# Block 1 of a fused attention and SwiGLU kernel: the sums of h move to another place in VectorE's queue

## The chip, the cores and the metric

The kernel runs on one core of a Trainium2 chip. The metric is device microseconds (us) of one execution. Eight runs of the kernel before lie between 1035.02 and 1037.15 us, with a median of 1036.09 us.

## The reference

Two layers follow each other. The first is linear attention without softmax over batch 8, 8 heads, 576 positions and a head width of 64; the second is a SwiGLU feed-forward layer on 4608 rows of width 512 with 1536 hidden columns. All numbers are float32.

```python
kv = np.einsum('bhsd,bhse->bhde', k, v)
out = np.einsum('bhsd,bhde->bhse', q, kv)
x = out / rms(out) * g_norm            # rows (b, s), columns (h, d)
g = x @ w_gate
return (g * (1 / (1 + np.exp(-g))) * (x @ w_val)) @ w_out
```

## The kernel before

The 4608 rows are cut into 9 blocks of 512 rows (n = 0 to 8). For each block the kernel computes the product for the hidden layer ("up"), then the product with w_out ("down"), while the attention of the next block is filled into the down stage. The inner dimensions are multiplied by Strassen's method in Winograd's form: seven products p = 1 to 7 of halves take the place of eight. Block 0 is multiplied plainly, block 1 by one level of the method (class Up, L573), and blocks 2 to 8 by two levels (class Inner, L638). The change concerns block 1 alone.

In block 1, the 12 tiles of hidden columns are taken in 6 pairs, j = 0 to 5. In this text p3(2) is product 3 of pair 2, and so on. One product is 8 matmuls of 128x256. Products collect in three kinds of PSUM bank (L519): b takes products 1, 6, 7 and 4, a takes 2, and c takes 5 and then 3 on top. The order on TensorE is written out by hand in `sequence` (L590): for pair j, products 1 and 5 come first, then 4 and 3 of the pair before, then 6, 2 and 7.

After each product, engines other than TensorE read the bank:

- after 1, 6 and 7, ScalarE copies b into a scratch tile "r" (L567, L571, L601)
- after 2, VectorE adds bank a to the scratch (L597)
- after 7, VectorE adds bank c, which then holds product 5, to U3 (L605). This add is called U3(j). Product 3 of the same pair adds on top of bank c, so p3(j) can't start before U3(j) has read the bank
- after 4, ScalarE applies Silu (L609) and GpSimd multiplies one half of h (L610), called h1(j)
- after 3, VectorE adds bank c to U2 (L613), called U2(j), and GpSimd multiplies the other half of h (L614), called h2(j). Then `h_sums` (L932) makes two VectorE instructions of 128x256: s1 = a21 + a22, which reads what h1(j) wrote, and a21 = s1 - a11, which also reads what h2(j) wrote. The two together are called sums(j).

The results of the sums are read in block 1's down stage alone. GpSimd also subtracts weight tiles for the pairs to come (`prepare`, L581): three tiles "t" of 128x512 for each pair, out of a pool of 9. And block 1 has a third task: the second level's weight leaves for blocks 2 to 8 are made here (`leaf_steps`, L807) and written to DRAM. These are some 28 steps for each pair, four behind each product (L964): VectorE subtractions and additions on t, wg and wv, each with both operands in SBUF, and DMAs issued by SyncE. A tile t goes back to GpSimd when the DMA of its leaf has landed. For the last two pairs the leaves of wg and wv are left to the down stage (L636).

The framework places each instruction in its engine's queue by priority (the order in which the program makes them) and by when it expects the operands; `tc.issue_after` keeps an instruction behind another one on the same engine. On the chip each engine works its queue strictly in order. The lambdas at L111, L112 and L113 issue every add, subtract and multiply, so the profile shows those lines and one has to go by the tiles: "h<-s,h" on VectorE is the second instruction of the sums, "h<-r" on GpSimd is h1 or h2, "r<-c,r" on VectorE is U2 or U3, and "c<-x,wv" on TensorE is product 3.

Of the kernel before, what the change touches and what calls it, by code (L numbers as in the profile page):

```python
# [18 lines left out]
def kernel(  # L19
# [41 lines left out]
    nc = tc.nc  # L61
# [11 lines left out]
    NP = NF // 2  # L73
# [37 lines left out]
    add = lambda e, o, a, b: e.tensor_tensor(out=o, in0=a, in1=b, op=OP.add)  # L111
# [7 lines left out]
    class Words:  # L119
# [12 lines left out]
        def __init__(self, src, shape):  # L132
            self.raw = ld_pool.tile([P, LD], U32, name="ld")[:, 0 : 2 * BLK]
            dst = self.raw.rearrange("p (a b) -> p a b", a=shape[0])
            self.sent = nc.sync.dma_start(out=dst, in_=src)
            self.shape = shape
            self.begun = False
# [435 lines left out]
    class Up(Quad):  # L573
# [25 lines left out]
        def after7(self):  # L599
            self.u3 = self.piece(2)  # L600
            copied = nc.scalar.copy(out=self.u3, in_=self.ps["b"])  # L601

            with tc.issue_after(copied.ins):
                nc.scalar.activation(out=self.s, in_=self.s, func=ACT.Silu)
            add(nc.vector, self.u3, self.ps["c"], self.u3)  # L605

        def after4(self):
            g = self.piece(3)
# [3 lines left out]
        def after3(self):  # L612
            add(nc.vector, self.u2, self.ps["c"], self.u2)  # L613
            mul(nc.gpsimd, self.h[:, :, 0:HB], self.s, self.u2)  # L614
            self.ffn.ended = self.ffn.h_sums(self.j, 1, nc.vector)

        def multiply(self, p):
            super().multiply(p)
# [301 lines left out]
    class Ffn:  # L920
        def __init__(self, n, att):
            self.n, self.att = n, att
            self.h = h_pool.tile([P, NF, BLK], F32, name="h")
            self.ps, self.leaf_room, self.ended = {}, None, None

            self.making, self.later, self.latest = [], [], []

# [215 lines left out]
```

## Time and profile before

| what | value |
|---|---|
| median of 8 runs | 1036.09 us |
| the profiled execution | 1036.78 us |
| its span in the trace | 1035.0 us |
| up stage of block 1 | 160.4 to 241.2 us of the span |
| TensorE's clock in the execution | 1.00 of full speed |
| VectorE in 160 to 245 us, waiting for GpSimd's h | 10.0 us, 5 times |

The page of a profile has the busy time of each engine, its share in 40 slices of the span, and the groups of instructions by line. The timeline view lists an engine's instructions in order of time: the start, the duration, engine, line, operation, tiles written and read, and in brackets the idle time before it with what ended that. The view of waits gives for each pair of waiter and releaser the total, the count and the longest, in us. VectorE is pipelined: where instructions don't depend on each other, the next starts some 0.08 us before the one before it ends, so the price of one is the distance between starts.

### The profile page before, as it was taken

Reading aid. Unit: us, or ns where it says so; the run is one execution under the profiler, and the core shown is the slowest. Engines: PE = TensorE matmul, PEld = TensorE weight load, DVE = VectorE, ACT = ScalarE, POOL = GpSimd, SP = SyncE. Lnnn points to the kernel's source line nnn. Section 1 sums busy time; section 2 is a strip of 40 time slices with the busy share of each in tenths; the row PEclk is TensorE's granted clock in tenths of the full one; section 3 lists DMA queues with packets and bytes.
Section 4 is the critical chain, followed back from the end, with each engine's and each line's share of the span. In section 5 each row is a group of like instructions: output and inputs, shape, how many; then the busy total and the mean of one; then the engine's idle time right before and its main releaser. Section 6 shows DMA issues by size and latency. Waiting matters only on the chain.

```text
span 1035.0 us, 21447 instructions
## 1 busy us (share of the span) xinstructions
PE 1014.8 (98%) x8586; PEld 904.9 (87%) x8586; DVE 695.8 (67%) x1184; ACT 231.8 (22%) x362; POOL 368.7 (36%) x280
## 2 busy tenths in 40 slices
PE   5999999999999999999999999999999999999998
PEld 4544688878899989998999899988999899989997
DVE  2999596886756856575666666674669466856661
ACT  2665111222212211212111112111212111211110
POOL 0000443444025612463156305640455136513670
PEclk9999999999999999999999999999999999999999
DMA  7689704674678556855686468736872766067601
GB/s 214 198 268 259 150 1 127 178 201 93 187 206 243 111 110 213 242 146 103 187 249 170 66 203 239 202 51 181 242 196 53 168 197 194 22 155 215 189 29 42
DMA packets 247876, 168.15 MB, mean 162 GB/s; under 512 B 124640, under 2 KB 215904, under 8 KB 247776
## 3 DMA queue, kind: packets, MB, share of 16 engines
q1 hardware_dynamic: 221280, 163.36, 57.6%
q10 hardware_dynamic: 26432, 3.41, 2.1%
q8 instruction: 68, 1.11, 0.4%
q14 instruction: 32, 0.26, 0.1%
q0 software_dynamic: 64, 0.00, 0.0%
HBM read 138.02 MB, written 22.41 MB: 155 GB/s over the span
## 4 chain that ended last, share of the span: by engine, by line
PE 91%; DVE 4%; DMA 2%; issue 1%; ACT 1%; POOL 0%; SPq 0%; DVEq 0%; POOLq 0%; ACTq 0%
PE b L706 25%; PE b L551 20%; PE c L706 13%; PE c L551 10%; PE a L706 6%; PE a L551 5%; PE b L1008 4%; PE c L1008 4%; PE m L316 1%; PE m L357 1%; DMA h<-in_v_dram 1%; DVE xi L112 1%; DVE r L112 1%; DVE r L111 1%; DMA w<-t 1%
## 5 line engine op out<-in xcount | busy, mean ns | idle before, releaser
L111 POOL TENSOR_TENSOR r<-r 128x256 f32<-128x256 f32 (+1 forms) x105 | 110.9, 1063 | 310.2 <-DVE r L111 233.1
L111 DVE TENSOR_TENSOR r<-b,r 128x512 f32<-128x512 f32 (+1 forms) x273 | 162.1, 606 | 64.9 <-PE b L706 59.6
L112 POOL TENSOR_TENSOR t<-wo 128x512 f32<-128x512 f32 x81 | 115.4, 1449 | 194.4 <-DVE wo L111 106.0
L111 DVE TENSOR_TENSOR r<-c,r 128x512 f32<-128x512 f32 (+1 forms) x179 | 108.5, 618 | 94.7 <-PE c L706 55.5
L706 PE MATMUL b<-x,t 128*128 128x128 f32 x1092 | 151.1, 275 | 0.0
L706 PEld LDWEIGHTS b<-x,t 128*128 128x128 f32 x1092 | 136.5, 192 | 0.7 <-DVE r L111 0.2
L111 DVE TENSOR_TENSOR r<-a,r 128x512 f32<-128x512 f32 (+1 forms) x99 | 62.5, 631 | 106.2 <-PE a L551 62.9
L706 PE MATMUL c<-xi,t 128*128 128x128 f32 x840 | 112.2, 275 | 0.4 <-DVE xi L111 0.4
L113 POOL TENSOR_TENSOR h<-r 128x1024 f32<-128x1024 f32 (+1 forms) x40 | 81.3, 2047 | 82.5 <-DVE r L111 77.0
L706 PEld LDWEIGHTS c<-xi,t 128*128 128x128 f32 x840 | 102.8, 192 | 0.5 <-DVE xi L111 0.5
L551 PE MATMUL b<-wo,h 128*128 128x256 f32 x432 | 99.4, 382 | 0.1
L551 PE MATMUL b<-t,h 128*128 128x256 f32 x432 | 96.9, 381 | 0.0
L551 PEld LDWEIGHTS b<-t,h 128*128 128x128 f32 x432 | 81.3, 190 | 11.3 <-issue 0.2
L551 PEld LDWEIGHTS b<-wo,h 128*128 128x128 f32 x432 | 79.9, 190 | 12.7 <-DVE h L113 2.5
L720 ACT COPY r<-b 128x512 f32<-128x512 f32 x63 | 36.9, 586 | 212.1 <-PE b L706 205.3
L706 PE MATMUL b<-xi,t 128*128 128x128 f32 x588 | 79.9, 276 | 0.0
L706 PEld LDWEIGHTS b<-xi,t 128*128 128x128 f32 x588 | 72.4, 192 | 0.1
L706 PE MATMUL b<-x,wg 128*128 128x128 f32 x336 | 52.7, 279 | 0.2 <-DVE x L112 0.2
L706 PE MATMUL b<-x,wv 128*128 128x128 f32 x336 | 51.3, 275 | 0.0
L551 PE MATMUL c<-t,s 128*128 128x256 f32 x216 | 48.3, 380 | 0.0
L551 PE MATMUL a<-wo,h 128*128 128x256 f32 x216 | 48.3, 379 | 0.0
L551 PE MATMUL c<-wo,h 128*128 128x256 f32 x216 | 48.1, 379 | 0.0
(136 smaller groups left out, 1574.8 us busy)
## 6 DMA issues: line engine op xcount, KB each, us to landing
t<-w SPq DMA_DIRECT2D x336, 256.0 KB, 3.5
out_dram<-r SPq DMA_DIRECT2D x17, 512.0 KB, 3.2
ld<-in_k_dram SPq DMA_DIRECT2D x26, 288.0 KB, 5.1
ld<-in_v_dram SPq DMA_DIRECT2D x26, 288.0 KB, 6.1
ld<-in_moe_w_gate_dram SPq DMA_DIRECT2D x12, 512.0 KB, 4.9
ld<-in_moe_w_val_dram SPq DMA_DIRECT2D x12, 512.0 KB, 4.5
ld<-in_moe_w_out_dram SPq DMA_DIRECT2D x12, 512.0 KB, 4.6
w<-t SPq DMA_DIRECT2D x18, 256.0 KB, 2.5
```

Of the source, the lines that this page charges most:

```text
L111: add = lambda e, o, a, b: e.tensor_tensor(out=o, in0=a, in1=b, op=OP.add)
L112: sub = lambda e, o, a, b: e.tensor_tensor(out=o, in0=a, in1=b, op=OP.subtract)
L113: mul = lambda e, o, a, b: e.tensor_tensor(out=o, in0=a, in1=b, op=OP.mult)
L316: nc.tensor.matmul(self.kv_ps[r][u * D : (u + 1) * D, g, :], lhsT=k[:, u, c, :], rhs=v[:, u, c, :], start=(c == 0), stop=(c == KT - 1),)
L357: self.multiplied = nc.tensor.matmul(self.ps[i][u][p : p + D, t, j, :], lhsT=self.qt[rows, 2 * i + t, j, p : p + D], rhs=kvs[b % 3][rows, ...
L551: nc.tensor.matmul(banks[e][:, e], lhsT=lhsT, rhs=rhs, start=first and i == 0 and (e == 0 or banks[0] is not banks[1]), stop=i == self.ste ...
L706: nc.tensor.matmul(ps[:, i, f], lhsT=self.weight(o, p, f), rhs=self.operand(o, p), start=first and (i, f) == (0, 0), stop=True, skip_group ...
L720: nc.scalar.copy(out=dst, in_=ps)
L1008: nc.tensor.matmul(t, lhsT=w[f // 2][:, i, P * (f % 2) : P * (f % 2 + 1)], rhs=x[:, i, of], start=(i == 0), stop=(i == NS - 1),)
```

## The change

In block 1, the sums of pairs 0 to 4 are no longer made behind U2(j). They are kept as a closure ("owed") and made when the next pair's U3(j+1) has been made, with `issue_after` to keep them behind it in VectorE's queue. The sums of pair 5 stay where they were. No instruction is added or left out; ten VectorE instructions of 128x256 move.

```diff
@@ class Up, after7
-            add(nc.vector, self.u3, self.ps["c"], self.u3)
+            added = add(nc.vector, self.u3, self.ps["c"], self.u3)
+
+            owed, self.ffn.owed = self.ffn.owed, None
+            if owed:
+                with tc.issue_after(added.ins):
+                    owed()
@@ class Up, after3
-            self.ffn.ended = self.ffn.h_sums(self.j, 1, nc.vector)
+            if self.j < NP - 1:
+                self.ffn.owed = lambda: self.ffn.h_sums(self.j, 1, nc.vector)
+            else:
+                self.ffn.ended = self.ffn.h_sums(self.j, 1, nc.vector)
@@ class Ffn, __init__
-            self.ps, self.leaf_room, self.ended = {}, None, None
+            self.ps, self.leaf_room, self.ended, self.owed = {}, None, None, None
```

## The prediction

> **What bounds the kernel now.** I read the page first, then TensorE's waits, then the timelines of TensorE, VectorE and GpSimd in block 1's up stage.
>
> ```profile
> PE 1014.8 (98%) x8586; PEld 904.9 (87%) x8586; DVE 695.8 (67%) x1184; ACT 231.8 (22%) x362; POOL 368.7 (36%) x280
> ```
>
> TensorE (PE) is busy 98% of the span. A change that leaves its matmuls alone can only win its idle time. The view of its waits over the whole span has one entry in the middle of the run that is worth anything; the larger ones are DMAs before 15 us:
>
> ```profile
> PE c L551 <- DVE r L111: 3.5, 3, 1.7
> ```
>
> Three waits of bank c for VectorE. TensorE's timeline places them:
>
> ```profile
> 196.38 1.89 PE L551 MATMUL c<-x,t 128*128 128x256 f32 x8
> 198.11 1.89 PE L551 MATMUL b<-x,t 128*128 128x256 f32 x8
> 201.74 1.99 PE L551 MATMUL c<-x,wv 128*128 128x256 f32 x8 [1.74 <-DVE r L111]
> 203.57 1.89 PE L551 MATMUL b<-x,wv 128*128 128x256 f32 x8
> ...
> 213.61 1.89 PE L551 MATMUL b<-x,t 128*128 128x256 f32 x8
> 216.18 1.99 PE L551 MATMUL c<-x,wv 128*128 128x256 f32 x8 [0.68 <-DVE r L111]
> ...
> 226.64 1.89 PE L551 MATMUL b<-x,t 128*128 128x256 f32 x8
> 229.66 1.99 PE L551 MATMUL c<-x,wv 128*128 128x256 f32 x8 [1.13 <-DVE r L111]
> ```
>
> They are p3(2), p3(3), p3(4), each behind its U3. Unhindered, products start 1.73 us apart (198.11 - 196.38). The three start 3.63, 2.57 and 3.02 us after p4, so 1.90, 0.84 and 1.29 late, and the product after each comes 1.83 later instead of 1.73. All three together: 4.03 + 3 x 0.10 = 4.33 us. **That is the most this change can give.**
>
> Why is U3 late? VectorE's timeline ahead of U3(2), the add at 201.00:
>
> ```profile
> 192.89 0.69 DVE L112 TENSOR_TENSOR xi<-wv 128x512 f32<-128x512 f32 x1
> 196.52 0.43 DVE L112 TENSOR_TENSOR h<-s,h 128x256 f32<-128x256 f32 x1 [2.93 <-POOL h L113]
> 196.86 0.42 DVE L112 TENSOR_TENSOR xi<-wv 128x256 f32<-128x256 f32 x1
> 197.19 1.49 DVE L112 TENSOR_TENSOR wg<-wg 128x256 f32<-128x256 f32 x1
> ...
> 201.00 0.69 DVE L111 TENSOR_TENSOR r<-c,r 128x512 f32<-128x512 f32 x1
> ```
>
> and GpSimd's (POOL) in the same time:
>
> ```profile
> 188.24 1.27 POOL L112 TENSOR_TENSOR t<-wg,wv 128x512 f32<-128x512 f32 x1 [5.85 <-DMA w<-t]
> 189.46 1.32 POOL L113 TENSOR_TENSOR h<-r 128x512 f32<-128x512 f32 x1
> 193.99 1.26 POOL L112 TENSOR_TENSOR t<-wg,wv 128x512 f32<-128x512 f32 x1 [3.22 <-DMA w<-t]
> 195.21 1.27 POOL L113 TENSOR_TENSOR h<-r 128x512 f32<-128x512 f32 x1
> ```
>
> sums(1) stands 2.93 us for h2(1), which stands in GpSimd's queue behind a t tile that waits for a DMA. The same happens to sums(3) (3.06 us, 223.39 to 226.45) and sums(4) (1.38). Sums(0) and sums(2) don't wait. So the stalls at p3(2) and p3(4) have such a wait ahead of them, and the one at p3(3) has not.
>
> **The price of GpSimd's presence.** While GpSimd runs, a VectorE instruction with both operands in SBUF stands still: the 128x128 add on t takes 0.29 us alone and 1.35 at 188.30, beside GpSimd's 188.24. Adds from PSUM don't mind: the 99 adds from bank a have 0.693 as their longest. Here lies the catch. In the 2.93 us that VectorE now idles, GpSimd is running (193.99 to 196.48, 2.49 us). Freed of the wait, VectorE meets GpSimd with SBUF work.
>
> The Trainium skill ("SBUF — State Buffer", section "Who interferes with whom") says that a VectorE instruction with two SBUF inputs contends with a GpSimd instruction that reads SBUF, that the loser blocks for the whole instruction, and that one with at most one SBUF input doesn't contend. The rows above agree. By the rule alone only the PSUM add escapes and each of the two idle spans is worth about a microsecond; worked through as below the total would be an estimated 2.5 us.
>
> **The change, step by step**, in distances of starts.
>
> *Moved work.* In the old place each of the two instructions costs 0.34 (191.18 to 191.52 and 196.52 to 196.86), 0.67 together. In the new one they follow each other and depend: 0.45 (as the wg pair at 182.92 and 183.37) + 0.34 = 0.79. It is the same work from another pair, so between two U3s the net is +0.12. The sums issue no DMA.
>
> *U3(1)*, at 185.65: only sums(0) leaves, so 0.67 earlier, 184.98. (sums(0)'s 1.50 us at 181.17 is GpSimd's; the next instruction inherits it.) Nothing is won yet: p3(1) at 187.75 ran without a gap.
>
> *U3(1) to U3(2)*, now 15.35: less 2.93 idle, plus 0.12, is 12.54. New: GpSimd's 2.49 us. At most the add from bank a (0.60) and one instruction between the two GpSimd ones (0.34) escape, so 1.55 to 2.49. U3(2) starts at 184.98 + 14.1 to 15.0 = 199.1 to 200.0; it lasts 0.69 and TensorE follows 0.06 later, so p3(2) starts at 199.8 to 200.8 instead of 201.74. **Gain 1.0 to 1.9, taken 1.4**, the middle: a GpSimd tile due at 197.01 falls into the same stretch either way.
>
> *U3(2) to U3(3)*, now 14.43 without any idle: five GpSimd instructions, all of them already in VectorE's way. Plus 0.12. TensorE needs 13.30 for the same way (7 x 1.73 + 1.21 for the kv products), so VectorE sets the pace and the stall at p3(3) does not go, it stays near 0.9. **Gain there 1.3 (0.9 to 1.8).** What was late by a wait is late by VectorE's own work.
>
> *U3(3) to U3(4)*, now 13.49 with 3.06 idle: again GpSimd runs in it (223.93 to 226.42, 2.49) and VectorE has 2.1 us left to do, of which 0.60 is a PSUM add: 1.55 to 2.49 again. Further gain 3.06 - 0.12 - that = 0.45 to 1.39, and no more than 1.29, when p3(4) is on time; taken 0.9. **Total 2.2 (1.35 to 3.1).**
>
> *U3(5)* has no stall to lose: it is done at 238.32, p3(5) runs at 239.40 unhindered. The 1.38 us is worth nothing. sums(4) now stand for 0.79 before the copy of q at 238.23 (L341); the next to need that is the product at 247.49, 8 us of cover; without that cover it would cost the 0.79.
>
> *Who waits behind the moved sums?* In VectorE's queue the leaves of p7 and p5, 0.12 later at most; through them SyncE's send of t, the DMA, GpSimd's next t, and h1, h2 behind it. h2 has no reader left but the sums themselves. h2(1) should end near 196.6 to 197 and its sum is due at about 200.6: over 3 us of cover; for pair 3 less, under 1 us, but nothing late follows there. The t tiles that TensorE reads are ready over 15 us ahead (GpSimd's 197.01 is for pair 5, from 223). SyncE's order stays.
>
> *Afterwards* TensorE has no gap over 0.12 us from 229.66 to 716 in its timeline, and its list of waits has under 1 us there, so a shift goes through to the end.
>
> **Sum:** 1036.78 - 2.2 = 1034.6 for the profiled execution, which is 0.69 above the median; for the median 1036.09 - 2.2 = **1033.9**. A measurement of this kernel can tell about 0.2% from no change, 2.07 us: my value lies just beyond it.
>
> **Rivals.**
> 1. *All the idle time is won* (over 3.1 us, up to 4.33: 1031.8). It takes GpSimd's instructions falling beside PSUM adds or between VectorE's. For: h2 is no longer awaited. Against: U3(2) to U3(3) has no idle now and is 1.1 us longer than TensorE's way. Chance 0.17.
> 2. *GpSimd and the planner take most of it.* The place of each step is the planner's, and U3(4) shows two leaf steps (0.54) put ahead of it. If freed time is filled so ahead of U3(2) as well, the low ends give 1.0 - 0.54 - 0.12 + 0.45 = 0.8: 1035.3. This is also what "the change doesn't do what it says" looks like: U3 isn't earlier. Chance 0.18.
> 3. *Slower: the wait moves along with the sums.* The h sum behind U3(2) waits for h2(1), held by the t tile's DMA. If that lands over 4 us later than now (its landing took 4.20; the longest of a w<-t here is 5.4), each further us delays U3(3). Price: the longest wait seen, 3.06, behind U3(2) and U3(3) each: p3(3) 3.06 - 1.3 = 1.8 late, p3(4) another 3.06 - 0.9 = 2.2, total +4.0: 1040.1. Chance 0.07.
>
> The forecast has 0.58, of which 0.35 lies beyond 2.07. So faster 0.35 + 0.17 = 0.52, within the bound 0.23 + 0.18 = 0.41, slower 0.07. The range, 1031.7 to 1035.5, takes in the forecast, rival 1 and the better half of rival 2.
>
> **What would show it.** VectorE's waits for POOL's h fall from 10 us to under 4 (pair 5's 1.16 and 1.39 stay). The SBUF instructions beside GpSimd's t and h2 of pairs 1 and 3 go from 0.4 to some 1.4 us. The wait at p3(3) stays over 0.5 us; p3(2)'s and p3(4)'s shrink below 1. It is wrong if the first wait stays over 1.2 us, if p3(3) runs on time (rival 1), or if "h<-s,h" shows an idle time over 2 us in its new place (rival 3).

## The result, and the profile after

The changed kernel takes 1032.84 us (median of 11 runs, 1032.02 to 1033.81) against 1036.24 us before (31 runs). The ratio is 0.9967, with a 95% interval of 0.9959 to 0.9975: **3.4 us less**, where 2.2 was forecast. The profiled execution took 1033.81 us, 2.97 less than the one of before; its span is 1032.0.

TensorE's waits in the changed kernel (waiter, releaser: total us, count, longest) have one wait of bank c for VectorE left, where there were three with 3.5 us in all:

```profile
PE c L551 <- DVE r L111: 0.7, 1, 0.7
```

Its timeline shows which one. (Start, duration, and in brackets the idle time.)

```profile
197.73 1.89 PE L551 MATMUL b<-x,t 128*128 128x256 f32 x8
199.46 1.89 PE L551 MATMUL c<-x,wv 128*128 128x256 f32 x8
...
211.22 1.89 PE L551 MATMUL b<-x,t 128*128 128x256 f32 x8
213.85 1.99 PE L551 MATMUL c<-x,wv 128*128 128x256 f32 x8 [0.73 <-DVE r L111]
...
224.31 1.89 PE L551 MATMUL b<-x,t 128*128 128x256 f32 x8
226.04 1.89 PE L551 MATMUL c<-x,wv 128*128 128x256 f32 x8
```

p3(2) and p3(4) follow 1.73 us after p4, on time. p3(3) is still 0.90 late, as it was (0.84).

The up stage of block 1, from the start of p1(0) to the start of p3(5), took 78.96 us and takes 75.61: 3.35 less. The rest of the difference in the two profiled executions lies outside the stage. The stage begins 0.37 earlier, since the first loads landed earlier; and a wait for a t tile at the start of block 6 (717 us before, 713 here) was 0.28 us before and 1.24 here. In the profiled executions of the experiments that wait lay between 0 and 1.0 us, with no order in it. The tables below therefore give the stage's length beside the median of all runs; the stage is that of the one profiled execution of each kernel.

VectorE's timeline ahead of U3(2), the add at 198.62, in the changed kernel:

```profile
191.61 0.68 DVE L111 TENSOR_TENSOR r<-c,r 128x512 f32<-128x512 f32 x1
192.21 1.02 DVE L112 TENSOR_TENSOR xi<-wv 128x512 f32<-128x512 f32 x2
193.14 1.49 DVE L112 TENSOR_TENSOR wg<-wg 128x256 f32<-128x256 f32 x1
194.67 1.37 DVE L111 TENSOR_TENSOR wg<-wg 128x256 f32<-128x256 f32 x1
195.96 0.68 DVE L111 TENSOR_TENSOR r<-a,r 128x512 f32<-128x512 f32 x1
197.27 0.69 DVE L112 TENSOR_TENSOR xi<-wg 128x512 f32<-128x512 f32 x1 [0.62 <-DMA w<-xi]
...
198.62 0.69 DVE L111 TENSOR_TENSOR r<-c,r 128x512 f32<-128x512 f32 x1
```

and GpSimd's in that time:

```profile
192.91 1.45 POOL L112 TENSOR_TENSOR t<-wg,wv 128x512 f32<-128x512 f32 x1 [2.82 <-DMA w<-t]
194.31 1.45 POOL L113 TENSOR_TENSOR h<-r 128x512 f32<-128x512 f32 x1
195.72 1.45 POOL L112 TENSOR_TENSOR t<-wv 128x512 f32<-128x512 f32 x1
```

The third of these, a t tile for pair 5, waited for a landing DMA before the change:

```profile
197.01 1.39 POOL L112 TENSOR_TENSOR t<-wv 128x512 f32<-128x512 f32 x1 [0.53 <-DMA w<-t]
```

Three things are to be seen. The sum that stood 2.93 us for h2(1) is gone from here. The two instructions on wg, some 0.42 us each when alone, now run beside GpSimd's t and h2 and take 1.49 and 1.37: the blocking that the prediction set against the idle time. (The first of them took 1.49 before as well, at 197.19 beside the third t tile; that tile now runs beside bank a's add and a wait.) And a wait that the prediction doesn't have came up: 0.62 us for the store of the tile xi.

### The profile page after: what moved, and what is told of

The parts are those of the page before. It is cut to its first block, busy times and chain, and to the rows that moved or that the text cites. A ratio compares the mean times of both kernels' runs of the same rounds, so it can differ in the third digit from the quotient of the medians.

```text
span 1032.0 us, 21450 instructions
## 1 busy us (share of the span) xinstructions
PE 1014.4 (98%) x8586; PEld 905.3 (88%) x8586; DVE 700.0 (68%) x1184; ACT 231.9 (22%) x362; POOL 369.9 (36%) x280
## 4 chain that ended last, share of the span: by engine, by line
PE 92%; DVE 3%; DMA 3%; issue 1%; ACT 1%; SPq 0%; DVEq 0%; ACTq 0%
PE b L714 26%; PE b L551 20%; PE c L714 13%; PE c L551 10%; PE a L714 6%; PE a L551 5%; PE b L1016 4%; PE c L1016 4%; PE m L316 1%; PE m L357 1%; DMA h<-in_v_dram 1%; DVE xi L112 1%; DVE r L112 1%; PE c L482 1%; DMA t<-w 1%
```

## The experiments

"Late" is the distance from p4 to p3 beyond 1.73 us. "Stage" is from p1(0) to p3(5). The ratios are to the kernel before, run beside it on the same chip (its medians there lie between 1035.90 and 1036.25); each interval reaches some 0.0008 to 0.0014 to either side, so that of pair 1 alone touches 1. An edit is shown against the changed kernel where nothing else is said.

| kernel | p3(2), p3(3), p3(4) late | stage | median us | ratio |
|---|---|---|---|---|
| before | 1.90, 0.84, 1.29 | 78.96 | 1036.24 | 1 |
| changed | 0, 0.90, 0 | 75.61 | 1032.84 | 0.9967 |
| pair 1 alone | 0.46, 1.56, 1.36 | 78.30 | 1035.32 | 0.9991 |
| pair 3 alone | 1.85, 0.19, 0 | 76.87 | 1034.52 | 0.9988 |
| pairs 0, 2, 4 | 1.33, 0, 0.76 | 76.91 | 1033.61 | 0.9981 |
| pairs 1, 3 | 0.33, 1.56, 0 | 76.71 | 1033.64 | 0.9980 |
| behind bank a's add | 0.32, 0.89, 1.54 | 77.68 | 1034.32 | 0.9983 |
| changed, three places in xi | 0.25, 0.89, 0 | 75.96 | 1033.26 | 0.9973 |
| pairs 1, 3, three places in xi | 0, 1.48, 0 | 76.20 | 1033.10 | 0.9971 |
| all sums behind U3(5) | 0, 0, 0 | 74.61 | 1031.92 | 0.9961 |
| sums on GpSimd | 1.23, 0.56, 0.08 | 76.79 | 1034.08 | 0.9981 |
| changed, h1 on VectorE | 0, 0, 0 | 74.75 | 1031.61 | 0.9959 |
| before, h2 on VectorE | 0, 0, 0 | 74.61 | 1031.72 | 0.9960 |
| all sums late, h1 on VectorE | 0, 0, 0 | 74.61 | 1031.83 | 0.9960 |

To read why, I split the way from one U3 to the next on VectorE into three parts, worked out from the timeline. *Idle* is what each gap has beyond 0.04 us. *Blocked* is what SBUF instructions took beyond the 0.29, 0.42 and 0.69 us that 128x128, 128x256 and 128x512 take undisturbed. *Work* is the rest.

| kernel | U3(1) to U3(2): work + blocked + idle | U3(2) to U3(3) |
|---|---|---|
| before | 9.37 + 3.09 + 2.89 = 15.35 | 9.25 + 5.19 = 14.44 |
| changed | 9.38 + 4.06 + 0.58 = 14.02 | 9.26 + 5.23 = 14.49 |
| pair 1 alone | 8.69 + 3.13 + 2.10 = 13.92 | 9.92 + 5.23 = 15.15 |
| pair 3 alone | 9.36 + 3.09 + 2.86 = 15.30 | 9.24 + 4.55 = 13.79 |
| pairs 0, 2, 4 | 10.04 + 3.09 + 2.34 = 15.47 | 8.57 + 4.73 = 13.31 |
| pairs 1, 3 | 8.70 + 2.03 + 3.07 = 13.79 | 9.92 + 5.23 = 15.15 |
| behind bank a's add | 9.36 + 2.60 + 2.37 = 14.33 | 9.25 + 5.24 = 14.49 |
| pairs 1, 3, three places in xi | 8.58 + 4.69 + 0 = 13.26 | 9.92 + 5.24 = 15.16 |
| changed, three places in xi | 9.25 + 5.13 + 0 = 14.38 | 9.26 + 5.23 = 14.49 |
| all sums behind U3(5) | 8.81 + 2.92 + 2.18 = 13.91 | 8.58 + 4.65 + 0.06 = 13.29 |
| sums on GpSimd | 8.70 + 5.09 + 0.52 = 14.31 | 8.57 + 5.52 + 0.06 = 14.15 |
| changed, h1 on VectorE | 9.98 + 3.11 + 1.40 = 14.49 | 9.87 + 3.69 = 13.55 |
| before, h2 on VectorE | 9.87 + 2.95 + 0.73 = 13.55 | 9.73 + 3.76 = 13.48 |

### The parts of the change, one by one

```diff
-            if self.j < NP - 1:
+            if self.j == 1:
```

> Only sums(1) is moved behind the next pair's U3; the sums of the other pairs stay where they were. Theory W (the wait of sums(1) for h2(1) is what p3(2) pays): the stall at p3(2) goes, about 1.8 us. Sums(1) then stand between U3(2) and U3(3) beside sums(2), 0.79 us more, so about 1.1 us of it are left at p3(3), and sums(3) still wait about 3 us for h2(3) ahead of p3(4). Total gain about 1.1 us, some 1035.0. Rival O (what helps is the shorter queue ahead of every U3, not the waits): a fifth of the whole 3.4 us, 0.7 us, with the stall at p3(2) shrunk by no more than that.

Measured: 1035.32, 0.7 less than before by the medians, the stage 0.66 shorter. The stall at p3(2) fell by 1.44, and most of that came back at p3(3), 0.72 later than before, as theory W has it. The total was rival O's (0.7, where W had 1.1), but by O the stall at p3(2) would have shrunk by no more than 0.7. And the wait was not simply gone. VectorE waited 2.1 us in the same place for something else:

```profile
DVE xi L112 <- DMA w<-xi: 2.1, 1, 2.1
```

```diff
-            if self.j < NP - 1:
+            if self.j == 3:
```

> Only sums(3) is moved. Theory W: the stalls at p3(2) (1.90) and p3(3) (0.84) stay, the one at p3(4) goes: gain 1.3 us, some 1034.9. Rival O: 0.7 us, and some stall is left at p3(4).

Measured: 1034.52, stage 2.09 shorter. p3(4) is on time, as W has it, but p3(3) lost 0.65 of its lateness too, and nothing of the program had changed on that way. VectorE's timelines of before and of this run, in this order:

```profile
206.91 1.51 DVE L112 TENSOR_TENSOR wv<-wv 128x256 f32<-128x256 f32 x1
208.34 0.68 DVE L111 TENSOR_TENSOR r<-c,r 128x512 f32<-128x512 f32 x1
208.94 0.41 DVE L111 TENSOR_TENSOR wv<-wv 128x256 f32<-128x256 f32 x1
```

```profile
206.39 0.41 DVE L112 TENSOR_TENSOR wv<-wv 128x256 f32<-128x256 f32 x1
206.72 0.68 DVE L111 TENSOR_TENSOR r<-c,r 128x512 f32<-128x512 f32 x1
207.32 0.89 DVE L111 TENSOR_TENSOR wv<-wv 128x256 f32<-128x256 f32 x1
```

and GpSimd's t tile there, before and in this run:

```profile
206.87 1.27 POOL L112 TENSOR_TENSOR t<-wg,wv 128x512 f32<-128x512 f32 x1 [0.70 <-PE a L551]
```

```profile
206.38 1.55 POOL L112 TENSOR_TENSOR t<-wg,wv 128x512 f32<-128x512 f32 x1 [0.73 <-PE a L551]
```

Before, GpSimd began 0.04 us ahead of the subtraction on wv, which then took 1.51. Here it began 0.01 ahead and took 1.55 instead of 1.27, while the subtraction took its 0.41: GpSimd stood. Its work then fell beside U2's add from PSUM, which kept its 0.68. That is 0.64 us less blocking ahead of U3(3), in this one execution; the medians, 1.5 us apart where the stages are 2.09 apart, don't show that every execution has it.

```diff
-            if self.j < NP - 1:
+            if self.j in (0, 2, 4):
```

> Only the sums of pairs 0, 2 and 4 are moved, whose waits cost nothing before. Theory W: sums(0) are exchanged for nothing at U3(2), p3(2) stays 1.9 late; sums(2) leave the queue ahead of U3(3), 0.67 less, so p3(3) gains about 0.5; the waits for h2(1) and h2(3) stay. Total gain 0.5 us at most, some 1035.7. Rival O: three fifths of the whole, 2.0 us, 1034.2.

Measured: 1033.61, stage 2.05 shorter. Here **theory W in its plain form fell**: these sums don't wait, and moving them gave as much as rival O said. p3(3) came on time because sums(2) left the way ahead of it (work 8.57) and 0.46 less was blocked (4.73 + 8.57 = 13.31). p3(2) gained 0.57, since sums(0) left the way ahead of U3(1), and behind it they fell into time that VectorE would have waited anyway: from U3(1) to U3(2) work is 0.67 more (10.04) and idle 0.55 less (2.34), while sums(1) still wait 2.38 us. I had counted that exchange as nothing. So the theory has to be: what counts is when each U3 comes, and all three parts make that, work, blocking and waiting. Work ahead of a wait is free, and a part that is taken away is only worth what the other two leave of it.

```diff
-            if self.j < NP - 1:
+            if self.j in (1, 3):
```

> Only sums(1) and sums(3) are moved, the two whose waits stand ahead of a stall. Theory W (waits for h2, then VectorE's work with GpSimd's blocking): p3(2) some 0.5 late as with pair 1 alone, p3(3) late by 0.8 to 1.6, since sums(1) and sums(2) both stand ahead of U3(3), p3(4) on time. Gain 2.0 to 2.7 us, 1034.0 to 1033.3. Rival O (each pair's move is worth the same): two fifths of 3.4, 1.4 us, 1034.9. Beside the run with pairs 0, 2 and 4 (a gain of 2.0) it shows whether the parts add up.

Measured: 1033.64, stage 2.25 shorter, inside W's expectation; p3(4) is on time, p3(2) 0.33 late, and p3(3) 1.56 late with two pairs' sums ahead of it. Rival O, which had the number with pair 1 and with pairs 0, 2 and 4, falls here (1.4 for 2.25) and with pair 3 alone (0.7 for 2.09). The parts don't add up: 2.25 for these two and 2.05 for the other three make 4.30, and all five together give 3.35.

### The place

```diff
@@ after2
-            add(nc.vector, self.s, self.ps["a"], self.s)
+            added = add(nc.vector, self.s, self.ps["a"], self.s)
+
+            owed, self.ffn.owed = self.ffn.owed, None
+            if owed:
+                with tc.issue_after(added.ins):
+                    owed()
@@ after7: the same lines taken out
```

> The sums of pairs 0 to 4 are moved, but behind the add from bank a of the next pair, so ahead of its U3 and behind the time at which h2 is ready. Theory W: no VectorE wait for h2 over 0.5 us, each U3 has one pair's sums (0.67 us) more in front than in the changed kernel: p3(2) about 0.5 late, p3(3) 0.7 later than in the changed kernel, so some 1033.5, a gain of 2.7. Rival O (the place behind U3 is what counts): the gain falls to 1 us or less, 1035.2 or more.

Measured: 1034.32, 1.7 less by the medians and a stage 1.28 shorter: between the two expectations, and W's was wrong about the waits. Bank a's add of pair 4 comes before h2(3) is done, so sums(3) waited 2.7 us there and p3(4) was 1.54 late. Ahead of U3(2) VectorE stood 2.4 us for the store of xi, which neither theory had. Standing behind U3 is worth something of its own: there the sums are late enough that none of them waits.

### The store of xi

The leaves of wg and wv are written to two places of the tile xi, one for each, and a place can be written again when its store has landed. Here they go round three places:

```diff
-                steps = leaf_steps(self.j, [(halves(wg), (1, 2)), (halves(wv), (6, 3))], ffn.leaf_room)
+                steps = []
+                for m, s in enumerate(((halves(wg), (1, 2)), (halves(wv), (6, 3)))):
+                    steps += leaf_steps(self.j, [s], ffn.leaf_room[:, 6 * ((2 * self.j + m) % 3) :])
```

> The changed kernel with the leaves of wg and wv written in turn to three places of the tile xi instead of two, so that the leaves of wg of pair 2 needn't wait for the store of those of pair 1 (0.62 us of VectorE in the changed kernel, landing at 197.2). Theory S (this store now sets U3(2), and VectorE's pace carries every delay on to p3(3)): U3(2) and U3(3) up to 0.6 earlier, p3(3) 0.3 late instead of 0.9: 1032.3. Rival: GpSimd's blocking takes the freed time, nothing moves, 1032.8.

Measured: 1033.26; the ratio, 0.9973, is inside the interval of the changed kernel's. The rival holds: VectorE's 0.58 us of idle went and blocking grew from 4.06 to 5.13, so that U3(2) came 0.36 later than in the changed kernel, and not earlier.

The same with the sums of pairs 1 and 3 alone moved (`if self.j in (1, 3):`):

> Only sums(1) and sums(3) moved, with the three places in xi as well. With the moved sums alone VectorE stood 3.1 us for the store of xi ahead of U3(2). Theory S: that wait goes, U3(2) comes 1.5 to 3 us earlier (GpSimd's blocking may take the rest), p3(2) is on time and p3(3), 1.56 late without this, by 0.5 or less: 1032.6 to 1031.7. Rival: the store is not what U3(2) waits for, p3(2) and p3(3) stay late, 1033.6.

Measured: 1033.10, the stage 0.51 shorter than without the places. Theory S is half right: the wait of 3.07 us went and p3(2) is on time, but of those 3.07 us 2.66 came back as blocking (2.03 to 4.69), so p3(3) stayed 1.48 late. Both runs show the same trade as the change itself: in VectorE's idle time GpSimd was running.

### What holds U3(3) back

```diff
@@ after7
-            owed, self.ffn.owed = self.ffn.owed, None
-            if owed:
+            if self.j == NP - 1:
                 with tc.issue_after(added.ins):
-                    owed()
+                    self.ffn.h_sums(0, NP - 1, nc.vector)
@@ after3
             if self.j < NP - 1:
-                self.ffn.owed = lambda: self.ffn.h_sums(self.j, 1, nc.vector)
+                pass
```

> The sums of pairs 0 to 4 are made in two instructions of 128x1280 behind U3(5), so no sums stand in VectorE's queue before that. Theory W (waits for h2 before; since the change, VectorE's own work plus GpSimd's blocking sets the pace between U3(2) and U3(3)): 0.79 us less ahead of U3(2) and 1.58 less ahead of U3(3), so the last stall, at p3(3), about 1 us with the restart, goes: 1031.9, or 0.999 of the changed kernel. The two large adds take some 2.9 us near 234 to 237, ahead of U2(5); the down stage needs h2(5) some 2.5 us later than it comes now, so that costs nothing. Rival D (the stall at p3(3) comes from a landing DMA or from ScalarE, not from VectorE's work): it stays, 1032.8, and the late adds may cost up to 1 us.

Measured: 1031.92 and a stage of 74.61, as W has it: the last stall is gone. VectorE's timeline at the end of the stage shows that the two large instructions had room, ahead of U2(5) at 236.61:

```profile
232.61 0.68 DVE L111 TENSOR_TENSOR r<-c,r 128x512 f32<-128x512 f32 x1
233.21 1.48 DVE L111 TENSOR_TENSOR s<-h 128x1280 f32<-128x1280 f32 x1
234.61 0.68 DVE L341 COPY r<-m 128x512 f32<-128x512 f32 x1
235.21 1.48 DVE L112 TENSOR_TENSOR h<-s,h 128x1280 f32<-128x1280 f32 x1
236.61 0.68 DVE L111 TENSOR_TENSOR r<-c,r 128x512 f32<-128x512 f32 x1
```

```diff
-                self.ffn.owed = lambda: self.ffn.h_sums(self.j, 1, nc.vector)
+                self.ffn.ended = self.ffn.h_sums(self.j, 1, nc.gpsimd)
```

> The sums of pairs 0 to 4 on GpSimd, behind h2, none on VectorE. Theory W with blocking: two GpSimd instructions of about 0.65 us each block VectorE for 1.3 us for each pair where it worked 0.79; U3(2) comes 0.5 later and U3(3) 1.0 later than in the changed kernel: 1033.6. Rival N (no blocking): VectorE has 0.79 less for each pair, the stall at p3(3) goes, 1031.9.

Measured: 1034.08, stage 1.18 longer than the changed kernel's. Taking the sums off VectorE made U3(1) 1.05 and U3(2) 1.34 us later in the stage than in the changed kernel: N, which had it faster, doesn't hold. From U3(1) to U3(2) work fell by 0.68 and blocked rose by 1.03. By place W was off, though: U3(2) was expected 0.5 later, and from U3(2) to U3(3), where another 0.5 was expected, the way is 0.34 shorter (work 0.69 less, blocked 0.29 more).

```diff
@@ after4, on top of the change
-            mul(nc.gpsimd, self.h[:, :, HB:BLK], g, self.u3)
+            mul(nc.vector, self.h[:, :, HB:BLK], g, self.u3)
```

> The changed kernel with h1 of block 1's pairs multiplied on VectorE (about 0.60 us each) instead of GpSimd (1.27 us each, in which VectorE's SBUF work stands still). Theory W with blocking: VectorE gains up to 0.6 us for each pair, the stall at p3(3) shrinks by 0.5 or more, 1032.3. Rival N (no blocking worth the name, VectorE is simply full): 0.6 us more for each pair, p3(2) is 0.4 late and p3(3) 1.2 later, 1034.4.

Measured: 1031.61, stage 74.75. VectorE has *more* to do and is earlier: between U3(2) and U3(3) work rose by 0.61 and blocked fell by 1.54, and U3(3) comes 0.85 us earlier in the stage (U3(2) 0.09 later). Rival N, 1034.4, is out. TensorE's timeline, where 0.73 us of idle stood:

```profile
211.06 1.89 PE L551 MATMUL b<-x,t 128*128 128x256 f32 x8
212.79 1.95 PE L551 MATMUL c<-x,wv 128*128 128x256 f32 x8
```

```diff
@@ after3, in the kernel before
-            mul(nc.gpsimd, self.h[:, :, 0:HB], self.s, self.u2)
+            mul(nc.vector, self.h[:, :, 0:HB], self.s, self.u2)
```

> The kernel before, with the sums in their old place, and h2 of block 1's pairs multiplied on VectorE, so that the sums wait for no GpSimd instruction behind a late t tile. Theory W: VectorE does 0.60 more for each pair and loses a blocking of 1.27; the waits of 2.93 and 3.06 go. U3(2) at about 199.3 and U3(3) at about 213.1, p3(2) and p3(3) some 0.3 late, p3(4) on time: a gain of 3.7 us, 1032.4. Rival O (the sums' place ahead of U3 is what costs): a gain under 1.5 us, 1034.7 or more.

Measured: 1031.72, stage 74.61: all of the 4.3 us, with the sums left where they were. So the sums in their old place make no stall by themselves; it took GpSimd in the way, at U3(2) by its queue (idle fell from 2.89 to 0.73) and at U3(3) by its blocking (5.19 to 3.76, against 0.48 more work). It is not the only remedy: making all sums late took the stalls away too, since what counts is when U3 comes. VectorE's timeline where the 2.93 us were:

```profile
192.49 0.68 DVE L113 TENSOR_TENSOR h<-r 128x512 f32<-128x512 f32 x1
193.09 0.68 DVE L112 TENSOR_TENSOR xi<-wv 128x512 f32<-128x512 f32 x1
193.69 0.41 DVE L112 TENSOR_TENSOR h<-s,h 128x256 f32<-128x256 f32 x1
```

The product takes 0.68 us in the place of 1.27, close ahead of its sum, and nothing waits there.

And the edits of the late sums and of h1 on VectorE together:

> Both of the last ideas together: the sums of pairs 0 to 4 behind U3(5) and h1 on VectorE. Theory W: no stall is left at any p3, as with the late sums alone, and VectorE has more to spare: 1031.8, the least that this stage allows (4.3 us below the kernel before). Rival N: p3(3) late again by about 0.6, 1032.5.

Measured: 1031.83, stage 74.61. As expected nothing is left to win here; the three kernels without a stall lie within 0.3 us of each other and of this one, and all of them have stages 0.86 to 1.00 us shorter than the changed kernel's. Their medians are about 1 us lower as well, but each interval of the ratio still takes in its 0.9967.

## Why the prediction was right, and where a size was off

- **The bound.** Three stalls, 4.33 us at most. Right: the four kernels without a stall have stages 4.2 to 4.35 us shorter, and none has more than that.
- **U3(1) to U3(2).** U3(1) came 0.68 us earlier in the stage, as worked out (0.67). From there the idle time goes and blocking comes in its place: right in kind. The size was off. I gave p3(2) 1.0 to 1.9 us and took 1.4; it won all of its 1.90. U3(2) came after 14.02 us, just under my 14.1 to 15.0. The two GpSimd instructions that I counted cost what the middle of my 1.55 to 2.49 says: 1.07 + 0.95 = 2.02 on the two instructions on wg. Three other terms were wrong. The third GpSimd instruction, at 197.01 before, I let cost the same "either way"; before, it cost 1.07 (the 1.49 at 197.19), and in the changed kernel it followed at once (195.72) and cost nothing, beside bank a's add and the wait for xi. That wait, 0.58 of idle, I didn't have. And the moved sums cost 0.01 more than in their old place instead of 0.12, since a leaf step was put between the two (185.20, 185.53, 185.86). So blocked rose by only 0.97, and with the 0.58 it makes 1.55, my lower end: that the sum met it is luck.
- **SyncE's order.** I had said that it stays. It doesn't: the loads of q, two together at 187.88 before, were split, and the next two stores of t went out at 188.17 and 190.26 instead of 189.64 and 191.50 (0.37 of that is the earlier stage). But this isn't needed for the third GpSimd instruction to follow at once. With pair 1 alone and with pairs 1 and 3 the order is the old one, with the second of these stores at 191.09 and 191.22, and the t tile starts right behind h2 all the same (196.20, 196.41): there the store landed 4.1 to 4.2 us after it was issued, before the change 5.4 us.
- **U3(2) to U3(3).** 14.43 + 0.12 was forecast, 14.49 measured, and the stall at p3(3) stayed at 0.90 (forecast: near 0.9). One term was mis-sized: TensorE's way from p3(2) to p3(3) is 13.49 us in the kernels without a stall (199.16 to 212.65 with all sums late), not 13.30, since going over to the kv products and back adds some 0.1 each. VectorE's way (14.43 before, 14.49 now) is thus 0.9 to 1.0 longer, and not 1.1. This is the step that a look at idle time alone would have missed, and the late sums and h1 on VectorE confirm its cause.
- **U3(3) to U3(4).** The further gain was taken at 0.9 with 1.29 as its cap; it was the cap, and with the restart of 0.10 more. Blocked rose by 1.53 (2.04 to 3.57), the low end of my 1.55 to 2.49, and work fell by 0.11 where 0.12 more was counted.
- **Sum.** 2.00 at p3(2), 1.39 at p3(4), -0.06 at p3(3): 3.33 (measured 3.35) instead of 2.2, and above the 3.1 at which the range of my sum ended. Twice I took the middle of a range whose low end came true. The two bounds, full blocking and all that can slip past it, came out nearly right; the choice between them was not argued from anything. By the Trainium skill's rule alone ("SBUF — State Buffer", section "Who interferes with whom") the prediction had 2.5; the rule's mechanism is what the runs show (1.49 and 1.37 beside GpSimd for 0.42), and its size here hangs on what VectorE happens to hold at that moment.
- **The rivals.** All idle time won: its number was met (over 3.1 us), its mechanism not, since p3(3) kept its stall and blocking rose by 0.97 and 1.53 us. What tells it from the forecast is the signs: the wait at p3(3) stayed at 0.73, those at p3(2) and p3(4) are gone, and the SBUF instructions beside GpSimd went to some 1.4 us. The planner refilling the time ahead of U3: it did not. The wait moving along with the sums: they waited for no h2 again; the view of VectorE's waits for POOL's h has 1.4 us left, all of it pair 5's. But a wait did come up in another place, the store of xi, which I hadn't priced: 0.62 us here, 2.1 with pair 1 alone, 3.1 with pairs 1 and 3, and 0.6 to 2.4 in six of the other kernels.
- **Afterwards.** The shift went through to the end, but for the t tile at the start of block 6, whose wait changes from run to run.

Two points stay open. Why the store of t landed sooner, so that the third GpSimd instruction followed at once, wasn't tried apart from the rest; what that gave of p3(2)'s 1.90, and what the new order on SyncE's queue gave, is read from timelines and not shown. And the stage's parts not adding up is explained by the three-part tables; no run held GpSimd's starts fixed.

## What to carry to other kernels

When an engine waits, look at what the other engines do in that time before the idle time is counted as a gain: here VectorE's waits lay under GpSimd's instructions, and taking a wait away turned about half of it into blocking (0.97 of 2.31 us ahead of U3(2), 1.53 of 3.02 ahead of U3(4)). Where VectorE and GpSimd share a stage, count a GpSimd instruction on SBUF data against VectorE's time too, and try the plain remedy first: here 0.60 us more on VectorE for 1.27 less on GpSimd, for each pair, gave 4.3 us with the place of the sums left alone. And a wait that is removed uncovers the next one in line, so name it before.

## What the runs showed of the hardware beyond what was expected

- Hundredths of a us decide who stands. In the traces of this case, among GpSimd instructions of block 1's up stage that begin after an idle time over 0.2 us and within 0.05 us of a VectorE instruction on SBUF data, VectorE's stood wherever GpSimd's record begins 0.012 us or more ahead (31 of 31), GpSimd's wherever it begins 0.001 ahead or later than VectorE's (16 of 16), and at 0.010 to 0.011 ahead either did (GpSimd's twice, VectorE's once). In the two cases shown above, a GpSimd instruction whose record begins 0.04 us ahead of a VectorE subtraction's cost VectorE 1.1 us; one that begins 0.01 us ahead stood itself until the subtraction was done and then cost 0.48, because an add from PSUM lay beside it.
- GpSimd was slowed too: its 128x512 took 1.27 us on a free stretch and up to 1.73 (before) and 1.66 (changed) beside VectorE's SBUF work.
- Stores of xi landed 3.1 to 5.3 us after they were issued, in the kernels before and changed; the one that VectorE stood for in the changed kernel is, by the order of the stores, the one issued at 191.89, some 7 us after its data were made (the step at 184.06), since the program has SyncE send the leaves in program order, behind others. It landed at 197.17.
